# Seven half products for two pairs of column tiles in batch 2's first product and for a second pair of row tiles in batch 0's second product, with w_out's scaling split over two engines

## The chip, the cores and the metric

The kernel runs on one core of a Trainium2 chip. The core has a matrix engine (TensorE, PE in the profile, with its weight loads as PEld), a vector engine (VectorE, DVE), a scalar engine (ScalarE, ACT), GpSimd (POOL) and an engine that mostly issues transfers (SyncE, SP). Each engine works through its own instructions in the order in which they were issued to it, and waits on semaphores for the others. PE writes to PSUM, DVE and ACT read it. The metric is the device time of one execution in microseconds, lower is better; a version counts as faster or slower when it differs by more than 2%.

## What is computed

Four batches of 768 positions, 8 heads of 64: a local attention (16 positions each way, plus 24 block summaries with the maximum of the keys and the mean of the values), and on its output, as 3072 rows of 512, a feed-forward layer with a swish whose slope is given per channel.

```
k_sum = k.reshape(B, H, nb, block, D).max(axis=3)
v_sum = v.reshape(B, H, nb, block, D).mean(axis=3)
scores_l = where(|i - j| < 16, scale * q @ k.T, -1e9)
scores_s = scale * q @ k_sum.T + log(block)
a = softmax(concat(scores_l, scores_s))
x = (a @ concat(v, v_sum)) as rows of 512        # 4 x 768 rows
h = x @ w_in                                     # 512 -> 2048: the first product
g = h * sigmoid(beta * h)
out = g @ w_out                                  # 2048 -> 512: the second product
```

## The kernel before

The kernel takes the batches one after the other. For a batch b it forms the attention (scores, exp on ACT, a mask on DVE, the product with the values, a division on DVE), turns the result into `xT` (512 channels as 4 groups of 128 rows by 768 positions), makes the first product into `h_sb` (16 column tiles of 128 by 768) with the swish on ACT, and then the second product, whose rows go out in tiles of 128. Everything is bf16 with sums in f32. `w_out_sb` is scaled once by 1/beta (`scale_w_out`, 16 pieces of 128x512), since ACT's Silu is given beta*h.

A full column tile of the first product is 8 matmuls of 384 positions (4 channel groups by 2 halves of the positions). `h_some` (operation `c` of the list LAST: tile, PSUM place, first and last channel group) issues them, and `cs` its Silu. A pair of column tiles can instead be made by seven half products in place of eight (`P`), each of two matmuls: sums of quarters of `xT` (`xs`, `x_sums`) and of quarters of `w_in_sb` (`ws`, `w_in_sums`, which also overwrites one quarter) take the place of the operands, and DVE puts the products together in PSUM (`p1`, `u2`, `u3`, `c22`, `c21`, `c12`). The dictionary SEVEN says for which pairs of which batch this is done. Before, these are the pairs 3 and 5 (column tiles 6, 7, 10 and 11) in batch 3 alone.

A row tile of the second product is either 16 matmuls of 512 columns (`o_atom`, four at a time, for batch 0's row tiles 0, 3, 4 and 1), or a pair of row tiles t and t+3 is made by seven half products of 8 matmuls of 256 columns (`half_products`, `product`, `gather`; batch 0's pair t=2, and all three pairs of the other batches). For these, `w_sums` forms sums of `w_out_sb` once, and `h_sums` (`hs`) sums of `h_sb` for each batch; DVE, ACT and POOL put the results together.

The order of the work is written out by hand. `main` is a list of steps of PE work: 8 pairs of column tiles of batch 0's first half (`h_two`), 16 tiles of its second half (`h_half`), the steps of its second product, and then for each later batch 16 steps of the first product (`h_step`, each a sixteenth of the list LAST) and 21 of the second. Everything else stands in the table AT, which gives each piece a place between the steps: loads (`kl`, `ql`, `vl`), DMA transposes on SP's queue (`kd`, `qd`), key windows and key maxima (`win`, `kx`, `ks`), scores (`sc`), masks (`mk`), the products with the values (`av`) and the transposes into `xT` on ACT's queue (`xd`). ENG says which engine makes a copy (d DVE, a ACT, p POOL). So the table fixes the order on each engine; how long a piece waits, it does not say.

PSUM has eight banks: `one` (two single ones), `big[1]` and `big[2]` (two banks each), and a pair that is `big[0]` in the first product and two single accumulators in the second.

## Time and profile before

| | us |
|---|---|
| median of 3 runs (207.07 to 209.65) | 207.76 |
| the profiled execution's own time | 207.91 |
| its span in the trace | 206.2 |
| PE busy | 198.1 |
| DVE busy | 139.0 |
| ACT busy | 126.8 |
| POOL busy | 79.4 |

The profile is of one execution. Its page gives the busy time of each engine, the span in 40 slices, the DMA queues, the chain of work that ended last, and the costliest groups of instructions; behind it stands the trace, which answers for stretches of time, tiles and engines. In the chain a row is the start, the time and the line; in a timeline, the start, the busy time, the engine, the operation with its operands and their count, and in brackets the idle time before it and what ended that.

### The profile page before, as it was taken

What the parts mean: (1) busy time and instruction counts of PE and PEld (TensorE: products, weight loads), DVE (VectorE), ACT (ScalarE), POOL (GpSimd) and SP (SyncE); (2) the same over time, 40 slices, a digit from 0 to 9 for tenths busy, and PEclk for the clock granted to TensorE, in tenths of its full rate; (3) what the DMA queues carried; (4) which work ended last, traced back from release to release, by engine and by line L of the source; (5) the groups of instructions that cost most, each with busy time, mean ns of one, the idle gap of its engine ahead of it and who ended that gap; (6) DMA issues with size and microseconds to landing.
All of it is one profiled execution on the core that took longest, in us unless ns stands there. A gap on an engine that the chain in (4) does not pass through costs nothing.

```text
span 206.2 us, 5853 instructions
## 1 busy us (share of the span) xinstructions
PE 198.1 (96%) x2420; PEld 139.5 (68%) x2424; DVE 139.0 (67%) x327; ACT 126.8 (61%) x197; POOL 79.4 (38%) x112
## 2 busy tenths in 40 slices
PE   7799999999999999999999999999999999999993
PEld 2577766665555775666887866657888866568882
DVE  4567555799979950779799522589789475797132
ACT  2279686588787116767986139668895457792210
POOL 7976992402970049600093379601201100000011
PEclk9999999999999999999999999999999999999999
DMA  6999999999996849999799999999524620000222
GB/s 115 186 172 196 207 206 203 206 193 156 141 180 78 205 98 157 147 137 150 127 185 116 181 153 195 155 156 167 116 105 110 151 103 0 0 3 0 102 101 105
DMA packets 86794, 28.17 MB, mean 137 GB/s; under 512 B 75232, under 2 KB 83824, under 8 KB 86768
## 3 DMA queue, kind: packets, MB, share of 16 engines
...
## 4 chain that ended last, share of the span: by engine, by line
PE 83%; DMA 7%; DVE 4%; issue 3%; POOL 2%; POOLq 0%
PE big L674 21%; PE one L755 15%; PE acc L755 10%; PE one L706 7%; PE one L674 5%; PE big L602 5%; DMA xT<-xn 4%; PE one L608 4%; DMA qrow<-in_q_dram 3%; PE big L462 3%; PE big L647 2%; PE big L415 2%; PE big L534 2%; PE big L608 2%; PE big L449 1%
## 5 line engine op out<-in xcount | busy, mean ns | idle before, releaser
L674 PEld LDWEIGHTS <-w_in_sb 128*128 128x128 bf16 x352 | 34.4, 98 | 22.9 <-issue 0.5
L674 PE MATMUL big<-xT,w_in_sb 128*128 128x384 bf16 x280 | 47.5, 326 | 0.3 <-DMA xT<-xn 0.3
L664 ACT ACTIVATE h_sb<-big,beta_sb 128x768 bf16<-128x768 f32 x39 | 34.6, 901 | 20.2 <-PE big L674 18.7
L736 POOL TENSOR_TENSOR o_sb<-p,u 128x256 f32<-128x256 f32 x10 | 7.3, 725 | 79.8 <-DVE u L736 59.9
L755 PEld LDWEIGHTS <-h_sb 128*128 128x128 bf16 x320 | 30.6, 98 | 4.5 <-issue 0.2
L755 PE MATMUL one<-w_out_sb,h_sb 128*128 128x256 bf16 x240 | 30.2, 273 | 0.2 <-ACT o_sb L393 0.2
L470 ACT ACTIVATE e<-big,bias 128x768 bf16<-128x768 f32 x32 | 27.3, 900 | 4.1 <-PE big L462 2.2
L755 PEld LDWEIGHTS <-s_sb 128*128 128x128 bf16 x240 | 23.2, 98 | 2.8
L736 DVE TENSOR_TENSOR u<-one,p 128x256 f32<-128x256 f32 x20 | 8.4, 422 | 18.1 <-PE one L755 18.0
L399 POOL COPY kw<-km 128x288 bf16<-128x288 bf16 x12 | 7.1, 596 | 34.2 <-DVE km L386 23.0
L253 POOL DMA_DIRECT2D ve<-in_v_dram x15 | 17.1, 1172 | 4.3 <-PE one L929 3.2
L706 PE MATMUL one<-w_out_sb,h_sb 128*128 128x512 bf16 x61 | 14.5, 380 | 0.4 <-issue 0.3
L474 DVE TENSOR_TENSOR e<-e,mask 128x768 bf16<-128x768 bf16 x24 | 12.9, 563 | 1.8 <-ACT e L470 1.6
L674 PE MATMUL one<-xT,w_in_sb 128*128 128x384 bf16 x72 | 14.0, 326 | 0.0
L393 ACT COPY o_sb<-one 128x256 f32<-128x256 f32 (+1 forms) x14 | 6.0, 432 | 12.6 <-PE one L755 7.8
L736 DVE TENSOR_TENSOR s_sb<-h_sb 128x768 bf16<-128x768 bf16 (+2 forms) x15 | 7.6, 508 | 9.2 <-ACT h_sb L682 7.1
L592 POOL DMA_DIRECT2D qn<-in_q_dram x16 | 13.4, 872 | 0.0
L592 POOL DMA_DIRECT2D kn<-in_k_dram x16 | 13.3, 856 | 0.0
L561 DVE TENSOR_TENSOR xn<-big,r 128x768 bf16<-128x768 f32 x12 | 11.5, 958 | 0.4
L386 DVE TENSOR_REDUCE km<-kT 128x24 bf16<-128x768 bf16 x12 | 11.2, 945 | 0.7 <-ACT kT L393 0.6
L602 PE MATMUL big<-xT,w_in_sb 128*128 128x384 bf16 x64 | 11.4, 326 | 0.0
L755 PE MATMUL acc<-t_sb,h_sb 128*128 128x256 bf16 x80 | 10.9, 273 | 0.0
...
## 6 DMA issues: line engine op xcount, KB each, us to landing
...
ve<-in_v_dram POOLq DMA_DIRECT2D x14, 208.0 KB, 12.7
...
```

The lines of the kernel that those rows point to most:

```text
L253: nc.gpsimd.dma_start(out=ve[:, g, 0:n, 0:D], in_=bass.AP(src.tensor, src.offset - W * D, [[D, P], [P * D, n], [1, D]]))
L470: nc.scalar.activation(out=e[:], in_=s[:, :, 0:HS], func=ACTF.Exp, bias=bias[:, 0:1], scale=scale)
L474: eng_of(ENG[f"mk{b}"][2 * g + u]).tensor_mul(out=e.rearrange("p h (m q) -> p h m q", q=QT), in0=e.rearrange("p h (m q) -> p h m q", q=QT) ...
L561: nc.vector.tensor_mul(out=x[:, 3 * us[0]:3 * us[0] + 3 * n].rearrange("p (k j) h d -> p k (j h) d", k=n), in0=tv[:, :, :, 0:D], in1=r[:, ...
L592: nc.gpsimd.dma_start(out=t[:, :, h], in_=pair(k if nm == "k" else q, b, g)[h].rearrange("(j p) d -> p j d", p=P))
L602: nc.tensor.matmul(t[:, 0:HS], w_in_sb[:, ki, i * P:(i + 1) * P], xT[:, ki, 0:HS], start=(ki == 0), stop=(ki == k1 - 1))
L608: nc.tensor.matmul(t[:, 0:HS], w_in_sb[:, ki, i * P:(i + 1) * P], xT[:, ki, lo:lo + HS], start=(ki == 0), stop=(ki == k1 - 1))
L664: nc.scalar.activation(out=h_sb[:, i, :].rearrange("p (k m) -> p k m", k=2), in_=t[:, :, 0:HS], func=ACTF.Silu, scale=beta_sb[:, i:i + 1])
L674: nc.tensor.matmul(o, w_in_sb[:, ki, i * P:(i + 1) * P], x, start=(ki == 0), stop=(ki == k1 - 1))
L706: nc.tensor.matmul(t[:, 0:hi - lo], h_sb[:, n, ms * P:(ms + 1) * P], w_out_sb[:, n, lo:hi], start=(n == 0), stop=(n == k2 - 1))
L736: eng.tensor_tensor(out=o, in0=a, in1=b, op=op)
L755: nc.tensor.matmul(SLOTS[n], a[:, j, t * P:(t + 1) * P], b[:, j], start=(j == 0 and n not in (2, 3, 7)), stop=(j == J2 - 1), skip_group_ch ...
```

## The change

Three things change, and with them most numbers of AT.

Batch 2's first product gets the pairs 3 and 5 by seven half products, as batch 3 has them. `w_in_sums`, which ran at the start of batch 3, moves into batch 1's list, behind column tile 12. LAST[2] is a new list, which also holds DVE's and POOL's work on the keys of batch 3 (`kw`, `kx`, `ks`, that stood in AT). The third sum of `h_sums` for batch 2 moves into its second product (`hz2`).

In batch 0's second product the row tiles 1 and 4 are no longer made by `o_atom`, but as a second pair (t=1) by seven half products. `h_sums` for batch 0 covers 256 columns in place of 128 and stands in eight pieces. Its result `s_sb` and OPERANDS are made at the start, since it is needed before the head's tiles are given back.

Of the 16 scalings of `w_out_sb`, 7 go to POOL. Some copies of batch 0 and 1 change their engine: one group of key windows, one `xT` copy and one query copy from DVE to ACT, two copies of key maxima from POOL to DVE.

```diff
-    'scale': [8.3, 16.158, 16.833, 21.634],
+    'scale': [14.35, 8.574, 20.331, 22.721],
...
-    'exp1': [23.6],
+    'exp1': [27.302],
...
-    'ks2': [57.494, 58.64, 61.796, 70.807],
+    'ks2': [62.273, 71.221, 58.389, 61.875],
...
-    'kw1': 'dddd', 'qt1': 'ddaa', 'x0': 'dd', 'ks1': 'pppp', 'scale': 'd' * 16, 'oc': 'aaaa',
+    'kw1': 'ddad', 'qt1': 'adaa', 'x0': 'ad', 'ks1': 'pddp', 'scale': 'dppdppdpddpddpdd', 'oc': 'aaaa', 'vm1':
...
     2: [
-        ('c', 0, 2, 0, 2), ('c', 2, 1, 0, 2), ('c', 3, 3, 0, 2), ('c', 1, 0, 0, 2), ('c', 0, 2, 2, 3),
...
+        ('c', 1, 2, 0, 2), ('c', 3, 1, 0, 1), ('xs', 3), ('c', 3, 1, 1, 2), ('c', 8, 3, 0, 2), ('c', 8, 3, 2,
+        3), ('c', 3, 1, 2, 3), ('c', 1, 2, 2, 3), ('xs', 0), ('c', 5, 0, 0, 1), ('c', 5, 0, 1, 2), ('c', 1, 2,
...
-SEVEN = {1: {}, 2: {}, 3: {3: (2, 1), 5: (0, 1)}}
+SEVEN = {1: {}, 2: {3: (2, 1), 5: (0, 1)}, 3: {3: (2, 1), 5: (0, 1)}}
...
+        elif name == "kw":
+            windows_nat(cp_of(ENG[f"win{b + 1}"][args[0]]), args[0])
+        elif name == "kx":
+            key_max_nat(args[0])
+        elif name == "ks":
+            key_sums(cp_of(ENG[f"ks{b + 1}"][args[0]]), args[0])
...
-    main.extend([lambda ms=ms, a=a: o_atom(0, ms, a) for ms in (0, 3, 4, 1) for a in range(4)])
-    products(0, (2,))
+    main.extend([lambda ms=ms, a=a: o_atom(0, ms, a) for ms in (0, 3) for a in range(4)])
+    products(0, (1, 2))
...
-    at("hs0", [lambda i=i: h_sums(0, J2, 2 * P, (i,)) for i in range(4)])
+    at("hs0", [lambda i=i, h=h: h_sums(4 * h, 4 * h + 4, P, (i,)) for h in range(2) for i in range(4)])
+    at("hz2", [lambda h=h: h_sums(4 * h, 4 * h + 4, 0, (2,)) for h in range(2)])
```

Batch 0's second product has eight steps of `main` with atoms fewer and seven with half products more, so batch 1 begins at step 46 in place of 47; most places of batches 2 and 3 move by one with it. One number of `ks2` changes what is computed: head pair 1's key maxima of batch 2 are copied into `kw` at 71.221, behind the scores that read them (66.132 and 66.349), so these scores use the 24 maxima that batch 1 left there.

Four places show how rows move on the engines. The first is ACT at the end of batch 0's first product: `qn` are batch 1's queries, `o_sb` a finished row tile, `e` the exponentials of the scores, and the table load with the dummy is the change to the exponential's table. Before:

```order
L826 ACT_TABLE_LOAD
L826 ACTIVATE dummy<-bias 128x1
L393 COPY qn_162<-big_82 128x768
L393 COPY qn_163<-big_82 128x768
L393 COPY o_sb<-one_75 128x512
L470 ACTIVATE e<-big_78,bias 128x768
L470 ACTIVATE e<-big_77,bias 128x768
```

On the same engine at the same place, after:

```order
L395 COPY qn_160<-big_77 128x768
L395 COPY qn_162<-big_82 128x768
L395 COPY qn_163<-big_82 128x768
L395 COPY o_sb<-one_75 128x512
L835 ACT_TABLE_LOAD
L835 ACTIVATE dummy<-bias 128x1
L472 ACTIVATE e<-big_78,bias 128x768
```

The table load moved behind the query copies and the first finished row tile, directly ahead of the first exponential.

The second place is DVE in the second half of batch 0's first product (`km` are key maxima, `t_sb` the sums of `w_out_sb`). Before:

```order
L382 TENSOR_REDUCE km_121<-kw_110 128x24
L362 TENSOR_SCALAR w_out_sb<-w_out_sb,inv_beta 128x512 x4
L382 TENSOR_REDUCE km_122<-kw_111 128x24
L362 TENSOR_SCALAR w_out_sb<-w_out_sb,inv_beta 128x512 x8
L382 TENSOR_REDUCE km_123<-kw_112 128x24
L382 TENSOR_REDUCE km_124<-kw_113 128x24
L736 TENSOR_TENSOR t_sb<-w_out_sb 128x2048
```

After:

```order
L384 TENSOR_REDUCE km_122<-kw_111 128x24
L398 COPY kw_111<-km_122 128x12x24
L364 TENSOR_SCALAR w_out_sb<-w_out_sb,inv_beta 128x512 x2
L384 TENSOR_REDUCE km_124<-kw_113 128x24
L364 TENSOR_SCALAR w_out_sb<-w_out_sb,inv_beta 128x512 x3
L745 TENSOR_TENSOR s_sb<-h_sb 128x4x256
L364 TENSOR_SCALAR w_out_sb<-w_out_sb,inv_beta 128x512 x3
L384 TENSOR_REDUCE km_123<-kw_112 128x24
L398 COPY kw_112<-km_123 128x12x24
L745 TENSOR_TENSOR t_sb<-w_out_sb 128x2048
```

Seven scalings are gone from it, two copies of key maxima and the first sum of `h_sb` stand between the others.

The third place is POOL in the same stretch; `ve` are batch 1's values, `kn` batch 2's keys. Before:

```order
L253 DMA ve<-in_v_dram 128x13x64 x4
L327 AFFINE_SELECT mask<-mask 128x64
L329 MEMSET mask 24x768
L399 COPY kw_110<-km_121 128x12x24
L399 COPY kw_111<-km_122 128x12x24
L399 COPY kw_112<-km_123 128x12x24
L399 COPY kw_113<-km_124 128x12x24
L592 DMA kn<-in_k_dram 128x6x64 x8
```

After:

```order
L255 DMA ve<-in_v_dram 128x13x64 x2
L364 TENSOR_SCALAR w_out_sb<-w_out_sb,inv_beta 128x512 x3
L255 DMA ve<-in_v_dram 128x13x64
L401 COPY kw_110<-km_121 128x12x24
L364 TENSOR_SCALAR w_out_sb<-w_out_sb,inv_beta 128x512 x2
L401 COPY kw_113<-km_124 128x12x24
L364 TENSOR_SCALAR w_out_sb<-w_out_sb,inv_beta 128x512 x2
L594 DMA kn<-in_k_dram 128x6x64 x8
```

The seven scalings stand between the loads and the copies, three of them ahead of the last load of values.

The fourth place is POOL in batch 1's second product; `kn` and `qn` are batch 3's keys and queries, the sums into `o_sb` belong to the row tile pairs t=0, 1 and 2. Before:

```order
L736 TENSOR_TENSOR o_sb<-p_1884,u_1936 128x256
L399 COPY kw_113<-km_124 128x12x24
L592 DMA kn<-in_k_dram 128x6x64 x6
L736 TENSOR_TENSOR o_sb<-p_2077,u_2177 128x256
L592 DMA kn<-in_k_dram 128x6x64 x2
L736 TENSOR_TENSOR o_sb<-p_2282,u_2311 128x256
L592 DMA qn<-in_q_dram 128x6x64 x8
```

After:

```order
L745 TENSOR_TENSOR o_sb<-p_1926,u_1978 128x256
L401 COPY kw_111<-km_122 128x12x24
L594 DMA kn<-in_k_dram 128x6x64 x4
L745 TENSOR_TENSOR o_sb<-p_2118,u_2216 128x256
L594 DMA kn<-in_k_dram 128x6x64 x4
L745 TENSOR_TENSOR o_sb<-p_2324,u_2353 128x256
L594 DMA qn<-in_q_dram 128x6x64 x8
```

Two of the loads of keys moved behind the sum of the pair t=1.

111 lines of the change are left out of this document (54 added, 57 removed), and 73 rows, old and new, of tables (ENG, LAST).

## The prediction

> **What bounds the kernel now.** I read the page first, then each stage by windows, the chain of waits, and the timelines of single engines at the places that the change touches.
>
> ```profile
> span 206.2 us, 5853 instructions
> PE 198.1 (96%) x2420; PEld 139.5 (68%) x2424; DVE 139.0 (67%) x327; ACT 126.8 (61%) x197; POOL 79.4 (38%) x112
> PE 83%; DMA 7%; DVE 4%; issue 3%; POOL 2%; POOLq 0%
> ```
>
> PE is busy for 96% of the span and carries 83% of the chain: time goes where PE loses or saves it. Two windows, batch 0's second product and batch 1's first, tell how much room the others have.
>
> ```profile
> 48.00:75.00 27.00, 26.61 (x406) 16.56 (x408) 24.19 (x46) 16.39 (x26) 9.95 (x12) 1.00 1.20 145
> 75.00:100.00 25.00, 25.00 (x188) 16.11 (x186) 14.87 (x31) 17.02 (x22) 11.78 (x14) 1.00 1.74 148
> ```
>
> The columns are the length, then PE, PEld, DVE, ACT and POOL busy, the granted clock (1.00) and DMA. From 48 to 75 us DVE works 24.19 of 27: it is almost as full as PE. From 75 to 100 it has 10 us free.
>
> **The work that PE is spared.** Rows of the chain of waits (start, time, line):
>
> ```profile
> 52.30 1.83 PE one L706 x8
> 54.13 0.46 PE big L462 x24
> ...
> 58.71 0.51 PE big L509 x28
> ...
> 72.71 1.75 PE one L755 x16
> ...
> 75.33 1.30 PE big L674 x8
> ...
> 114.85 7.99 DMA xT<-xn
> ...
> 125.64 15.60 PE big L674 x96
> ...
> 164.31 0.65 PE one L674 x4
> ...
> 184.48 0.77 PE acc L755 x7
> ```
>
> A matmul of 512 columns (L706) takes 1.83/8 = 0.229 us, one of 256 (L755) 1.75/16 = 0.109, one of the first product (L674) 15.60/96 = 0.1625. Row tiles 1 and 4 of batch 0 cost 32 x 0.229 = 7.32 us; as seven half products they cost 56 x 0.109 = 6.12. That spares 1.20. Two pairs of column tiles are 32 matmuls; by seven half products 28, which spares 4 x 0.1625 = 0.65. That such pairs can run without holes is seen in batch 3: from 164.31 to 184.48 are 20.17 us, and 124 x 0.1625 = 20.15. So the most that these edits can spare PE is 1.85 us.
>
> **Batch 2's start: the 0.65 is waited away.** The timeline of PE there:
>
> ```profile
> 119.82 1.46 PE L674 MATMUL big<-xT,w_in_sb 128*128 128x384 bf16 x8
> 121.12 0.81 PE L674 MATMUL one<-xT,w_in_sb 128*128 128x384 bf16 x4
> 121.77 0.81 PE L674 MATMUL big<-xT,w_in_sb 128*128 128x384 bf16 x4
> 122.88 2.11 PE L674 MATMUL big<-xT,w_in_sb 128*128 128x384 bf16 x12 [0.29 <-DMA xT<-xn]
> ```
>
> PE does 16 matmuls that need channel groups 0 and 1 alone, 2.60 us, and then waits 0.29 for the third group's transpose, the one of 7.99 us in the chain. The new list has 12 such matmuls (tiles 1, 3 and 8) ahead of the first that needs group 2: 12 x 0.1625 = 1.95. The transpose comes out of batch 1's second product, whose steps keep their places to one another, so it lands as long after that product's start as before, and the wait becomes 0.29 + 0.65 = 0.94. Behind the landing both lists have the same PE work, 128 - 16 = 124 - 12 = 112 matmuls. So this edit counts -0.65 and +0.65.
>
> What it adds on DVE is covered, by these groups (DVE's additions in PSUM, and one of the four `w_in_sums` in the timeline):
>
> ```profile
> L736 DVE TENSOR_TENSOR big<-big,o_sb 128x384 f32<-128x384 f32 x6 | 3.4, 565 | 0.6 <-PE big L647 0.5
> ```
>
> ```profile
> 164.78 0.42 DVE L736 TENSOR_TENSOR wsum<-w_in_sb 128x512 bf16<-128x512 bf16 x1
> ```
>
> The sums of `xT` (`xs`) need all four groups and hold DVE's queue until these have landed; behind them stand the sums of the first pair, whose products come later still, and the Silu of tiles 1, 3, 8 and 5 are on ACT, so nobody waits for the held queue. Two pairs need ten additions of 0.57 in PSUM, and with batch 3's keys and the sums of `h_sb` DVE is full for nearly the whole stage. Batch 3 has a like list without a hole: I take 0, between 0 and the 1.1 of two additions by which it may come late. The moved `w_in_sums`, 4 x 0.42, fall into the 10 us that DVE has free from 75 to 100: 0, and at most their 1.7.
>
> **Batch 0's second product: the 1.20 is partly given back.** ACT around its table load:
>
> ```profile
> 49.55 1.28 ACT L826 ACT_TABLE_LOAD   x1
> 50.84 0.20 ACT L826 ACTIVATE dummy<-bias 128x1 f32<-128x1 f32 x1
> ...
> 54.16 0.58 ACT L393 COPY o_sb<-one 128x512 f32<-128x512 f32 x1 [0.33 <-PE one L706]
> 54.65 1.70 ACT L470 ACTIVATE e<-big,bias 128x768 bf16<-128x768 f32 x2
> ```
>
> The load of 1.28 us stood in time in which ACT waited for PE anyway. Now it stands behind the copy of the first row tile: 54.16 + 0.58 + 1.28 + 0.20 = 56.2, and the first exponential ends at 57.1 (0.85 each). PE comes to the third scores, which need its PSUM, at 54.13 + 0.46 + 8 x 0.229 + 0.51 = 56.9. It waits about 0.3. Bounds: 0, and 1.28 for the whole load; the small end is nearer, since both times are summed from rows.
>
> DVE in the same stage, and the two rows of POOL that stood beside it:
>
> ```profile
> 40.21 1.13 DVE L362 TENSOR_SCALAR w_out_sb<-w_out_sb,inv_beta 128x512 bf16<-128x512 bf16 x4
> 41.26 2.68 DVE L396 COPY kw<-big 128x960 bf16<-128x960 bf16 x4
> ...
> 44.71 1.31 DVE L362 TENSOR_SCALAR w_out_sb<-w_out_sb,inv_beta 128x512 bf16<-128x512 bf16 x4
> ...
> 50.79 1.21 DVE L736 TENSOR_TENSOR t_sb<-w_out_sb 128x2048 bf16<-128x2048 bf16 x1
> 51.92 1.80 DVE L396 COPY qn<-big 128x768 bf16<-128x768 bf16 x2
> ...
> 72.20 0.68 DVE L736 TENSOR_TENSOR h_sb<-h_sb 128x1024 bf16<-128x1024 bf16 x1
> 72.80 0.42 DVE L736 TENSOR_TENSOR u<-one,p 128x256 f32<-128x256 f32 x1
> ...
> 74.95 0.84 DVE L736 TENSOR_TENSOR o_sb<-acc,u 128x256 f32<-128x256 f32 x2
> ```
>
> ```profile
> 44.93 0.42 POOL L399 COPY kw<-km 128x288 bf16<-128x288 bf16 x1 [6.48 <-DVE km L382]
> ...
> 50.93 1.36 POOL L399 COPY kw<-km 128x288 bf16<-128x288 bf16 x1 [0.43 <-DVE km L382]
> ```
>
> Ahead of the first `t_sb`, DVE loses seven scalings of 0.28 (2.0) and one of two groups of key windows (1.3), and gains a sum of `h_sb` (0.6) and two copies of key maxima (POOL's 0.42 each at most; 0.3 by my estimate). So it starts about 2.1 us earlier. From there to `u` of the pair t=2 it gains four sums (2.4, at 0.60 from start to start) and the gathering of t=1 (0.42 + 0.42 + 0.84), and loses a query copy (0.9): about 3 more. So `u` ends near 73.2 - 2.1 + 3 = 74.1, or up to 2 us earlier if DVE no longer waits for anybody in this stretch: 72.1 to 74.1, by the middle 73.1. PE needs it for the last but one product of t=2, two products (1.75 us) ahead of batch 1, at 75.33 - 1.20 + 0.3 - 1.75 = 72.7. That is a wait of 0.4 (0 to 1.4). [...] Of POOL's seven scalings three stand beside DVE's copies out of PSUM, two beside its reductions, two beside scalings. I add 0.18 for each of the last two, but half of that, since some of DVE's lost time comes out of waits: 0.2, and 0.6 for DVE in all.
>
> POOL's scalings are also ahead of the last load of values and of batch 2's keys in POOL's queue. Those loads land late anyway; the last one of values, issued at 36.2:
>
> ```profile
> ve<-in_v_dram POOLq DMA_DIRECT2D x1, 208.0 KB, 16.5
> ```
>
> With 16.5 us it waited in the queue behind weights and queries, so some us of later issue leave its landing where it was: 0.
>
> **The sum.** 207.91 - 1.20 - 0.65 + 0.65 + 0.3 + 0.6 = 207.6 for an execution such as the profiled one, which lies 0.15 above the median of the runs: 207.4.
>
> **The rivals.**
>
> *All of it comes.* The transposes into `xT` around 155 to 161 us, with no loads of keys beside them, landed so:
>
> ```profile
> DMA to landing us min/median/max: 2.7/2.8/3.5
> ```
>
> And those of batch 1's second product so:
>
> ```profile
> DMA to landing us min/median/max: 3.1/5.5/8.0
> ```
>
> If the third one lands 1 us earlier, the 0.65 and the 0.29 come back: 206.4; with DVE and ACT on time too, 205.6. Against it: nothing beside the transposes gets lighter.
>
> *The transposes land later: slower.* POOL's rows there:
>
> ```profile
> 113.02 0.72 POOL L736 TENSOR_TENSOR o_sb<-p,u 128x256 f32<-128x256 f32 x1 [3.46 <-issue]
> 113.70 1.69 POOL L592 DMA_DIRECT2D kn<-in_k_dram  x2
> ```
>
> Two loads of keys (1.69 us of issuing) ran beside the third transpose, issued at 114.85; now four do. If the two more hold it up by their own length, batch 2 starts 1.7 later: 207.4 + 1.7 = 209.1. It decides from 0.4 us on, where the 207.8 of before is passed. For it: the transposes are slow only where these loads are.
>
> *POOL's scalings block DVE whole: slower.* A scaling on POOL lasts about 0.75 us by its copy (0.42/288 x 512). If the four beside DVE's reductions and scalings each hold DVE for that long, 3.0 us in place of 0.2, DVE is the bound there: 207.4 + 2.8 = 210.2. It decides from 0.15 us each on. [...]
>
> *It does nothing in sum:* ACT and DVE give back the whole 1.20: 207.8, inside the forecast's own range.
>
> **How the numbers follow.** The forecast, with its own range of 206.5 to 208.4 (both waits 0; DVE's at 1.4), gets 0.5; all of it comes 0.2; late transposes 0.15; blocked DVE 0.1; 0.05 for what I don't see, such as keys or queries of batch 2 that land late in their new order. The time is that of the likeliest, 207.4. To hold it 8 times in 10 the range takes in most of the first rival and the late transposes: 205.8 to 209.3. A measurement of this kernel can tell about 2% (4.2 us) from no change. Faster by that is 203.6, below all that PE is spared: 0.02. Slower by that is 211.9, both slower rivals at once: 0.03. Within: 0.95.
>
> **What would show it.** In the changed kernel's profile: 32 matmuls fewer in the atoms' group and a batch 0 that ends 0.3 to 0.9 earlier; batch 2's first product with a wait of about 0.9 for `xT` after 12 matmuls and no hole behind it; holes of some tenths on PE between 56 and 73 us that end with ACT's `e` and DVE's `u`. The forecast is wrong if the third transpose lands within 6 us of its issue or takes over 9, if PE's busy time falls by less than 1.5 us, or if DVE's scalings and sums between 43 and 50 us grow by more than 1 us in all.

## The result and the profile after

The changed kernel takes 217.91 us in the median of 4 runs (215.39 to 218.97), the kernel before 208.0 beside it: 1.0427 times as long, with a 95% interval of 1.0302 to 1.0551. It is slower, and lies outside the range of the prediction (205.8 to 209.3). Ratios, here and in the table below, leave out the executions that are over 1.5% above the fastest of their kernel, such as the 218.97 here, while medians are of all. The profiled execution took 217.34 us. The page of the changed kernel:

```profile
span 215.6 us, 5914 instructions
PE 200.8 (93%) x2440; PEld 142.7 (66%) x2444; DVE 147.9 (69%) x332; ACT 128.9 (60%) x204; POOL 89.4 (41%) x118
...
PE 49%; DVE 22%; DMA 18%; issue 4%; POOL 3%; ACT 1%; SPq 0%; ACTq 0%; POOLq 0%; DVEq 0%
```

PE was busy for 96% of the span and is now busy for 93%; of the chain of waits it carried 83% and now carries 49%. So PE waits, and DVE and transfers have come into the chain. Where, the windows tell, cut at the first matmul of each stage. For before (length, then PE, PEld, DVE, ACT and POOL busy, clock, DMA):

```profile
48.93:75.17 26.24, 25.87 (x402) 16.28 (x405) 23.43 (x42) 15.58 (x24) 10.06 (x13) 1.00 1.15 144
...
95.97:119.82 23.85, 23.31 (x389) 19.82 (x388) 18.38 (x42) 15.61 (x27) 9.29 (x13) 1.00 1.18 155
119.82:141.08 21.26, 20.97 (x131) 12.51 (x128) 10.88 (x21) 14.52 (x18) 12.71 (x16) 1.00 1.80 162
141.08:164.15 23.07, 23.07 (x390) 19.65 (x388) 17.82 (x43) 16.69 (x27) 3.04 (x6) 1.00 0.68 132
```

And the same four stages after (batch 0's second product, batch 1's second, batch 2's first and second):

```profile
48.67:78.11 29.44, 27.13 (x425) 19.18 (x428) 26.65 (x52) 15.94 (x24) 9.36 (x12) 0.94 0.98 121
...
98.91:126.42 27.51, 24.97 (x390) 20.56 (x388) 21.76 (x50) 15.90 (x27) 8.80 (x12) 0.94 0.81 130
126.42:149.97 23.55, 20.79 (x126) 12.11 (x124) 15.12 (x27) 14.63 (x22) 14.77 (x18) 1.00 1.85 161
149.97:173.56 23.59, 23.48 (x390) 19.75 (x388) 20.44 (x42) 15.49 (x27) 1.49 (x3) 1.00 0.64 117
```

They are longer by 3.20, 3.66, 2.29 and 0.52, together 9.7. The first of them began 0.26 earlier, and the span grew by 9.4. Two of the four also have a granted clock of 0.94. The other stages are as long as before. PE's waits of over 1 us in them, from the timeline of PE (in brackets the wait and what ended it):

```profile
56.02 0.48 PE L464 MATMUL big<-qn,kw 64*128 64x64 bf16 x12 [1.87 <-DVE qn L398]
...
103.36 0.53 PE L464 MATMUL big<-qn,kw 64*128 64x64 bf16 x24 [2.54 <-DVE kw L398]
...
129.96 0.48 PE L676 MATMUL one<-xT,w_in_sb 128*128 128x384 bf16 x2 [1.42 <-DMA xT<-xn]
...
141.01 0.49 PE L649 MATMUL big<-e,w_in_sb 128*128 128x384 bf16 x2 [1.15 <-ACT h_sb L666]
```

The waits in batch 0 and 1 cost more than their length. Windows of 2 us (the same columns) show the clock at half for some 4 us behind each:

```profile
56.00:58.00 2.00, 1.65 (x15) 0.76 (x15) 2.00 (x4) 1.58 (x3) 1.14 (x2) 0.52 1.57 224
58.00:60.00 2.00, 2.00 (x33) 1.00 (x32) 1.01 (x4) 0.00 (x0) 0.00 (x0) 0.63 1.78 200
...
104.00:106.00 2.00, 2.00 (x11) 1.40 (x10) 1.93 (x6) 1.44 (x2) 0.00 (x0) 0.50 0.59 135
106.00:108.00 2.00, 2.00 (x14) 1.53 (x13) 1.57 (x4) 0.37 (x1) 0.00 (x0) 0.68 0.45 106
```

**What is late in batch 0.** Rows of DVE's timeline after, up to the query copy:

```profile
39.95 0.71 DVE L364 TENSOR_SCALAR w_out_sb<-w_out_sb,inv_beta 128x512 bf16<-128x512 bf16 x1
...
44.33 1.70 DVE L364 TENSOR_SCALAR w_out_sb<-w_out_sb,inv_beta 128x512 bf16<-128x512 bf16 x2
...
46.81 1.46 DVE L364 TENSOR_SCALAR w_out_sb<-w_out_sb,inv_beta 128x512 bf16<-128x512 bf16 x3
...
48.80 1.31 DVE L364 TENSOR_SCALAR w_out_sb<-w_out_sb,inv_beta 128x512 bf16<-128x512 bf16 x3
...
51.35 1.16 DVE L745 TENSOR_TENSOR t_sb<-w_out_sb 128x2048 bf16<-128x2048 bf16 x1
52.61 2.48 DVE L745 TENSOR_TENSOR t_sb<-w_out_sb,t_sb 128x2048 bf16<-128x2048 bf16 x2
55.02 0.95 DVE L398 COPY qn<-big 128x768 bf16<-128x768 bf16 x1
```

Nine scalings took 5.18 us where 9 x 0.28 = 2.5 was DVE's price before, and two sums of 1.24 stand ahead of the copy that PE waits for: the second scores go to the PSUM bank in which the transposed queries still lie. POOL's row beside them gives 1.56 us for one scaling:

```profile
37.40 4.68 POOL L364 TENSOR_SCALAR w_out_sb<-w_out_sb,inv_beta 128x512 bf16<-128x512 bf16 x3 [0.56 <-DMA w_out_sb<-in_moe_w_out_dram]
```

**What is late in batch 1.** The chain of waits (start, time, line) and, below, SP's own queue in the timelines, before and after:

```profile
91.29 0.86 DVE km L388
...
92.18 5.86 DMA kT<-kn
...
98.07 0.46 DVE kw L398
...
103.36 0.53 PE big L464 x24
```

```profile
77.35 4.69 SPq L596 DMA_TRANSPOSE kT<-kn  x3
```

```profile
80.56 12.84 SPq L598 DMA_TRANSPOSE kT<-kn  x3
93.56 3.75 SPq L598 DMA_TRANSPOSE qn<-qn  x2
97.36 1.28 SPq L598 DMA_TRANSPOSE kT<-kn  x1
```

```profile
SPq L598 <- DVE s_sb L745: 9.5, 1, 9.5
```

Three transposes of keys take 4.69 us on SP before and 12.84 after. In the table of waits one of them waits 9.5 us for DVE. The cause stands in the change's numbers: pair 1's maxima (`kx2`, 51.576) come ahead of its transpose (`kd2`, 52.012). So the reduction at 91.29 reads the old keys, the transpose may overwrite them only afterwards, and everything behind it on SP is late.

The order also changes more of what is computed than the one number of `ks2` named above. Pair 1's maxima are taken from the keys that `kT` still holds, and the copies of pairs 2 and 3 (`ks2` 58.389 and 61.875) stand ahead of their reductions (`kx2` 58.488 and 61.978), so they take the maxima that batch 1 left. POOL makes three of the four copies in one go, where DVE's reductions of these two pairs follow only at 101.24 and 104.99:

```profile
91.06 1.25 POOL L401 COPY kw<-km 128x288 bf16<-128x288 bf16 x3
```

### The profile page after: what moved, and what is told of

Read it like the earlier page. It is cut to its first block, busy times and chain, and to the rows that moved or that the text cites. A ratio compares the mean times of both kernels' runs of the same rounds, so it can differ in the third digit from the quotient of the medians.

```text
span 215.6 us, 5914 instructions
## 1 busy us (share of the span) xinstructions
PE 200.8 (93%) x2440; PEld 142.7 (66%) x2444; DVE 147.9 (69%) x332; ACT 128.9 (60%) x204; POOL 89.4 (41%) x118
## 4 chain that ended last, share of the span: by engine, by line
PE 49%; DVE 22%; DMA 18%; issue 4%; POOL 3%; ACT 1%; SPq 0%; ACTq 0%; POOLq 0%; DVEq 0%
PE one L764 13%; DMA kT<-kn 10%; PE acc L764 9%; PE big L604 5%; DVE s_sb L745 5%; PE one L676 4%; DMA qrow<-in_q_dram 3%; PE big L676 3%; DVE kw L398 3%; DMA qn<-in_q_dram 2%; DVE w_out_sb L364 2%; DMA xT<-xn 2%; PE big L649 2%; PE one L714 2%; DVE km L388 2%
## 5 line engine op out<-in xcount | busy, mean ns | idle before, releaser
L676 PEld LDWEIGHTS <-w_in_sb 128*128 128x128 bf16 x320 | 31.3, 98 | 22.3 <-issue 2.0
L666 ACT ACTIVATE h_sb<-big,beta_sb 128x768 bf16<-128x768 f32 x35 | 30.8, 901 | 19.9 <-PE big L676 15.3
L676 PE MATMUL big<-xT,w_in_sb 128*128 128x384 bf16 x216 | 37.5, 326 | 0.1
L764 PEld LDWEIGHTS <-h_sb 128*128 128x128 bf16 x352 | 33.6, 98 | 4.9
L764 PE MATMUL one<-w_out_sb,h_sb 128*128 128x256 bf16 x264 | 33.4, 273 | 0.0
L676 PE MATMUL one<-xT,w_in_sb 128*128 128x384 bf16 x104 | 20.3, 326 | 1.4 <-DMA xT<-xn 1.4
L388 DVE TENSOR_REDUCE km<-kT 128x24 bf16<-128x768 bf16 x12 | 11.2, 946 | 10.2 <-DMA kT<-kn 9.2
L684 ACT ACTIVATE h_sb<-one,beta_sb 128x384 bf16<-128x384 f32 x26 | 14.0, 582 | 1.7 <-PE one L676 1.5
L764 PE MATMUL one<-t_sb,s_sb 128*128 128x256 bf16 x88 | 12.3, 286 | 0.0
L764 PE MATMUL acc<-t_sb,s_sb 128*128 128x256 bf16 x88 | 12.3, 286 | 0.0
L764 PE MATMUL acc<-w_out_sb,s_sb 128*128 128x256 bf16 x88 | 11.4, 273 | 0.0
## 6 DMA issues: line engine op xcount, KB each, us to landing
ve<-in_v_dram POOLq DMA_DIRECT2D x14, 208.0 KB, 8.6
```

The lines of the kernel that those rows point to most:

```text
L388: nc.vector.tensor_reduce(out=km[g][:, NK:NK + nb], in_=kT[g][:, W:W + S].rearrange("p (n f) -> p n f", f=block), op=ALU.max, axis=AX.X)
L666: nc.scalar.activation(out=h_sb[:, i, :].rearrange("p (k m) -> p k m", k=2), in_=t[:, :, 0:HS], func=ACTF.Silu, scale=beta_sb[:, i:i + 1])
L676: nc.tensor.matmul(o, w_in_sb[:, ki, i * P:(i + 1) * P], x, start=(ki == 0), stop=(ki == k1 - 1))
L684: nc.scalar.activation(out=h_sb[:, i, kk * HS:(kk + 1) * HS], in_=one[kk][:, 0, 0:HS], func=ACTF.Silu, scale=beta_sb[:, i:i + 1])
L764: nc.tensor.matmul(SLOTS[n], a[:, j, t * P:(t + 1) * P], b[:, j], start=(j == 0 and n not in (2, 3, 7)), stop=(j == J2 - 1), skip_group_ch ...
```

## The experiments

The stages as in the windows above, and the medians (before as measured beside each, 207.9 to 208.2):

| kernel | batch 0, 2nd | batch 1, 2nd | batch 2, 1st | batch 2, 2nd | median | ratio, 95% |
|---|---|---|---|---|---|---|
| before | 26.24 | 23.85 | 21.26 | 23.07 | 208.0 | |
| after | 29.44 | 27.51 | 23.55 | 23.59 | 217.9 | 1.030 to 1.055 |
| kd_first | 30.75 | 23.49 | 22.45 | 23.59 | 215.0 | 1.022 to 1.037 |
| ws_behind_q | 28.29 | 25.45 | 23.21 | 23.59 | 215.9 | 1.024 to 1.040 |
| scale_dve | 28.00 | 24.80 | 22.37 | 23.59 | 213.5 | 1.018 to 1.031 |
| undo_seven2 | 27.98 | 27.15 | 21.56 | 23.35 | 214.4 | 1.022 to 1.038 |
| only_batch0 | 28.09 | 23.26 | 22.21 | 23.07 | 212.9 | 1.011 to 1.026 |
| mend_batch0 | 26.70 | 23.25 | 22.66 | 23.07 | 209.8 | 1.003 to 1.011 |
| nomask_batch0 | 26.23 | 23.24 | 21.77 | 23.07 | 208.7 | 0.998 to 1.006 |
| pairs_batch0 | 26.70 | 23.25 | 23.05 | 24.05 | 210.2 | 1.004 to 1.016 |
| only_keys2 | 26.24 | 24.98 | 22.66 | 23.07 | 211.0 | 1.009 to 1.021 |
| only_seven2 | 26.24 | 23.26 | 23.60 | 23.55 | 211.7 | 1.010 to 1.022 |
| seven2_keys_out | 26.24 | 23.26 | 25.94 | 24.42 | 212.3 | 1.015 to 1.027 |
| seven2_nokeys | 26.23 | 23.26 | 21.57 | 23.40 | 208.5 | 0.999 to 1.004 |
| seven2_keys_last | 26.24 | 23.25 | 22.02 | 30.05 | 216.0 | 1.031 to 1.041 |
| seven2_mended | 26.24 | 24.63 | 20.19 | 29.97 | 214.2 | 1.022 to 1.030 |
| seven2_fit | 26.24 | 23.83 | 20.69 | 24.41 | 209.1 | 1.003 to 1.008 |
| kl3_alone | 26.24 | 23.76 | 21.63 | 23.06 | 209.3 | 1.001 to 1.006 |
| mend_all | 26.69 | 30.05 | 25.49 | 24.42 | 218.7 | 1.037 to 1.049 |

The stages are of one profiled execution each.

### First, one thing at a time undone in the changed kernel

**kd_first.** The key transpose ahead of the maxima that read it:

```diff
-    'kd2': [46.896, 52.012, 49.287, 53.919],
+    'kd2': [46.896, 51.5, 49.287, 53.919],
```

> The changed kernel with one number moved: head pair 1's key transpose for batch 2 (kd2) at 51.5 instead of 52.012, so that it is issued ahead of the key maxima of the same pair (51.576). The order on every engine stays the same; what changes is who waits: before this edit the transpose on SP's queue waits for DVE's read of the old keys, and the maxima of that pair are those of batch 0's keys. Theory C (this wait holds SP's queue for 9.5 us and makes batch 1's second product late): the third key transpose is issued near 83 us instead of 93, DVE's wait of 2.54 for the key windows and PE's 2.54 for the scores at 103.4 vanish, with the half clock behind it; the kernel takes 217.9 - 2.5 to 3.7 = 214.2 to 215.4. Rival (DVE has too much in batch 1's first product: w_in's sums and the sums of h_sb crowd out the windows): DVE's queue stays as late, PE still waits over 1.5 us, and the time stays above 216.5.

215.02 us (213.54 to 215.83). SP's queue and PE at the place, from its timelines:

```profile
82.59 4.52 SPq L598 DMA_TRANSPOSE kT<-kn  x3
```

```profile
58.49 0.50 PE L464 MATMUL big<-qn,kw 64*128 64x64 bf16 x12 [3.26 <-DVE qn L398]
...
103.39 0.53 PE L464 MATMUL big<-qn,kw 64*128 64x64 bf16 x24 [0.18 <-DMA qn<-qn]
```

The three transposes are out by 87.1, and PE's 2.54 became 0.18. Batch 1's second product takes 23.49, less than before the change, and the time is in theory C's range. So one number, and the wait that it made on SP, is the whole loss of this stage: theory C holds. The other row tells that batch 0's wait differs from run to run with the same instructions: 1.87, here 3.26.

**ws_behind_q.** Two sums of `w_out_sb` behind the query copy:

```diff
-    'ws': [23.767, 23.768, 24.034, 31.733],
+    'ws': [23.767, 25.6, 26.6, 31.733],
```

> The changed kernel with the second and third sum of w_out (ws) at 25.6 and 26.6 instead of 23.768 and 24.034, as before: the second copy of batch 1's queries stands behind one of these sums on DVE instead of three. Theory B (the order on DVE: two sums of 1.24 us ahead of the copy that frees the bank for the second scores): PE's wait of 1.87 at 56 us falls under 0.4, the clock stays at 1.00 from 56 to 60 us, and the kernel takes 217.9 - 1.9 to 3.6 = 214.3 to 216.0. Theory A (POOL's scalings are what makes DVE late): the wait moves to what stands behind, and the time falls by less than 1: over 216.9.

215.89 us (214.06 to 218.4), at the upper end of theory B's range. The wait for the query copy is gone, but two new ones have come at 66 us, and batch 0's stage is still 28.29 us:

```profile
66.40 0.22 PE L536 MATMUL big<-ve,e 128*64 128x65 bf16 x1 [0.70 <-DVE e L476]
68.08 0.22 PE L536 MATMUL big<-ve,e 128*64 128x65 bf16 x1 [1.30 <-DVE e L476]
```

These are the masks, DVE's next work, which now has the two sums ahead of it. So the wait for the copy was made by the order, but two waits of together 2.00 took its place. That the time lies in theory B's range is in part luck: the profiled execution gains 1.15 us in batch 0 and 2.06 in batch 1's second product, which the edit doesn't touch. There PE waits 2.15 for the same copy of key windows, and its clock stays at 1.00 behind it.

**scale_dve.** No scaling on POOL:

```diff
-    'scale': 'dppdppdpddpddpdd'
+    'scale': 'dddddddddddddddd'
```

> The changed kernel with all 16 scalings of w_out on DVE. DVE gets seven scalings of 0.28 (2.0 us) back and loses what POOL's cost it: its own nine scalings took 5.2 us instead of 2.5. Theory A (POOL's scalings make DVE late): t_sb starts 1 us earlier or more, the wait at 56 us falls by as much, and the time falls by 1 to 3 us: 214.9 to 216.9. Theory B (the order on DVE makes it late): t_sb starts within 1 us of 51.35, PE still waits 1.0 to 2.7 us, and the time stays within 1 us: 216.9 to 218.9.

213.54 us (213.11 to 214.7), faster than either theory said. The first sum of `w_out_sb` starts at 51.98, 2.2 us behind the stage's start (after: 2.7, before: 1.9), and PE still waits:

```profile
56.58 0.35 PE L489 MATMUL big<-qn,kw 64*128 64x64 bf16 x12 [1.33 <-DVE qn L423]
```

By t_sb and the wait theory B is right, by the time neither. Its 16 scalings take DVE 5.19 us, as long as the nine beside POOL's (5.18): what POOL took off it, POOL cost it again. Much of the rest is the clock, which stays at 1.00 in all four stages of the profiled execution. Batch 0's second product is 1.44 us shorter, batch 2's first 1.18, and batch 1's second 2.71, where PE's wait for the key windows is 1.49 in place of 2.54 and no half clock follows:

```profile
101.96 0.53 PE L489 MATMUL big<-qn,kw 64*128 64x64 bf16 x24 [1.49 <-DVE kw L423]
```

The transpose on SP is held there too (three take 11.93 us), so this part of the gain is no sign for either theory.

**undo_seven2.** Batch 2's first product as before:

```diff
-SEVEN = {1: {}, 2: {3: (2, 1), 5: (0, 1)}, 3: {3: (2, 1), 5: (0, 1)}}
+SEVEN = {1: {}, 2: {}, 3: {3: (2, 1), 5: (0, 1)}}
...
-    'win3': [],
+    'win3': [90.341, 92.68, 90.196, 99.991],
```

> The changed kernel with batch 2's first product made as before (no half products, the old list, batch 3's keys at their old places, w_in's sums back in batch 3), everything else as changed. Theory D (the new list costs 2.8 us from batch 2's start to its end, where it was to cost nothing): 217.9 - 2 to 3.5 = 214.4 to 215.9, with no wait on PE from 131 to 150 us and one of about 0.3 to 0.8 for xT. Rival (what is lost there is handed down from batch 1, whose transposes come late): the time stays above 217.

214.44 us (213.95 to 216.15), in theory D's range. In the profiled execution batch 2's two products are 1.99 and 0.24 shorter than after the change, and PE waits 0.44 for `xT`; another 1.46 is gained in batch 0, which the edit doesn't touch. So the third part costs by itself, at its own place, about 2.2 us.

### Then, one part alone on the kernel before

In these kernels (and in mend_batch0, nomask_batch0, pairs_batch0, seven2_keys_out, seven2_nokeys and seven2_keys_last) batch 3's four key loads stand one step later against the steps of batch 1, as in the change; kl3_alone, below, prices that. The diffs show the main lines of each edit only.

**only_batch0** (second pair, its places and engines), **only_keys2** (the numbers of batch 2's keys, queries and values) and **only_seven2** (batch 2's first product):

```diff
-    main.extend([lambda ms=ms, a=a: o_atom(0, ms, a) for ms in (0, 3, 4, 1) for a in range(4)])
-    products(0, (2,))
+    main.extend([lambda ms=ms, a=a: o_atom(0, ms, a) for ms in (0, 3) for a in range(4)])
+    products(0, (1, 2))
```

```diff
-    'kd2': [47.896, 48.564, 50.287, 53.981],
-    'kx2': [50.116, 57.618, 60.611, 66.447],
+    'kd2': [47.896, 53.012, 50.287, 54.919],
+    'kx2': [49.237, 52.576, 59.488, 62.978],
```

```diff
-SEVEN = {1: {}, 2: {}, 3: {3: (2, 1), 5: (0, 1)}}
+SEVEN = {1: {}, 2: {3: (2, 1), 5: (0, 1)}, 3: {3: (2, 1), 5: (0, 1)}}
```

> The kernel before with the first part of the change alone: batch 0's second pair with its places, engines and the split scaling; the keys of batch 2 at the places of before and batch 2's first product as before. If batch 0's second product is what it was in the changed kernel (28.0 to 30.8 us from its first matmul to batch 1's, where 26.24 stood before) and the rest is as before, the time is 208.0 + 1.8 to 4.5 = 209.8 to 212.5. If the loss there comes from what else was changed, it is under 209.

> The kernel before with the second part alone: the numbers of batch 2's keys, queries and values (ql2, vl2, kd2, win2, kx2, ks2, qd2, vo2, exp2) as in the changed kernel; batch 0 and batch 2's first product as before. As in the changed kernel the key maxima of pair 1 are taken ahead of its transpose (from batch 0's keys), those of pairs 2 and 3 are copied ahead of their reduction, and pair 1's copy comes behind its scores. Theory C (the transpose on SP waits for that read and holds SP's queue): SP's third key transpose stands 6 to 10 us behind the second, DVE waits 1.5 us or more for the key windows behind it, batch 1's second product takes 24.8 to 27.5 us (before 23.85), and the kernel 208.2 + 1.0 to 3.7 = 209.2 to 211.9. Rival (it takes w_in's sums on DVE in batch 1 as well): 207.9 to 208.9.

> The kernel before with the third part alone: batch 2's first product with two pairs of column tiles by seven half products, its new list with batch 3's keys in it, w_in's sums moved into batch 1's list. My prediction counted this at nothing. In the three runs above where it stood, batch 2's first product took 22.4 to 23.2 us (before 21.26) and its second 23.59 (before 23.07). Theory D (the list itself costs it): 208.0 + 1.1 to 2.5 = 209.1 to 210.5, with a wait of 0.9 to 1.5 for the third group of xT. If it is only hurt by what batch 1 hands down late: 207.7 to 208.6.

212.89 (+4.7), 210.96 (+3.1) and 211.66 us (+3.4) against before beside them. Each part alone takes longer than before: the three intervals lie above 1, though none wholly above 2%. The first and the third are over the range that was given, the second is inside theory C's. The three sum to 11.2; since all hold the later key loads (0.7, below), twice 0.7 goes off: 9.8, where the whole change costs 9.9. So no loss is seen that only the parts together make, as far as medians of four runs tell. In only_keys2 SP's three transposes take 11.61 us, in only_seven2 PE waits thus:

```profile
134.43 0.48 PE L673 MATMUL big<-e,w_in_sb 128*128 128x384 bf16 x2 [1.60 <-ACT h_sb L690]
```

DVE's rows ahead of it tell why: a window copy waits 1.96 us for its key transpose, and the two sums in PSUM that ACT needs stand behind it.

```profile
131.54 0.57 DVE L422 COPY kw<-kT 128x1152 bf16<-128x1152 bf16 x1 [1.96 <-DMA kT<-kn]
132.03 0.93 DVE L412 TENSOR_REDUCE km<-kT 128x24 bf16<-128x768 bf16 x1
132.89 1.01 DVE L769 TENSOR_TENSOR big<-big,o_sb 128x384 f32<-128x384 f32 x2
```

The profiled run of only_batch0 was its fastest (209.97; the others 212.8 to 213.0), so its stages show only some 2 us of the loss.

### Batch 0: order, volume, or PE itself

**mend_batch0**, on only_batch0:

```diff
-    'ws': [23.767, 23.768, 24.034, 31.733],
+    'ws': [23.767, 25.6, 26.6, 31.733],
...
-    'exp1': [27.302],
+    'exp1': [23.8],
...
-    'qt1': 'adaa',
+    'qt1': 'aaaa',
...
-    'scale': 'dppdppdpddpddpdd',
+    'scale': 'dddddddddddddddd',
...
-    'vm1': 'dddd',
+    'vm1': 'dada',
```

> The run above with DVE relieved: all scalings on DVE again (no POOL scalings beside it), the second and third sum of w_out behind the query transposes, all four query copies and half of the copies of the means on ACT, and the exponential's table loaded ahead of the query copies. Theory V (DVE's volume bounds batch 0's second product: it was busy 26.2 of 28.0 us): about 1.5 us of DVE work leave, the stage takes 26.2 to 27.0 us, and the kernel 208.0 to 208.8. Theory B (only the order of the query copy made the loss): the stage takes about 25.3, PE's work alone, and the kernel 207.1.

**nomask_batch0**, on that:

```diff
-        at("mk" + n, [lambda g=g, u=u, b=b: mask_e(b, g, u) for g in range(G) for u in range(2)])
+        if b > 1:
+            at("mk" + n, [lambda g=g, u=u, b=b: mask_e(b, g, u) for g in range(G) for u in range(2)])
```

> The run above without the eight multiplications of batch 1's exponentials with the mask (left out: batch 1's local window is not cut to 16 positions on each side). DVE is spared 8 x 0.5 = 4 us between 55 and 73 us. Theory V: batch 0's second product loses its last waits and takes 25.0 to 25.6 us, so the kernel is 0.6 to 1.8 faster than the run above and 0.5 to 1.2 faster than before. Rival (what is left of the loss is PE's own, from changing more often between scores, products and values): the stage stays within 0.4 us of the run above.

The stage takes 26.70 us in mend_batch0, in theory V's range; the kernel, 209.8, is over it, and in its trace PE also loses 0.9 in batch 1's first product, where it waits for `xT`. nomask_batch0 leaves out the masks of batch 1's local attention, so it computes something else. There the stage takes 26.23, where V said 25.0 to 25.6 and the rival no change of more than 0.4: 0.47 shorter, nearly as the rival has it. Its window shows that nobody but PE is left:

```profile
51.25:77.48 26.23, 25.94 (x428) 18.60 (x428) 21.00 (x40) 16.34 (x27) 7.28 (x10) 1.00 0.95 126
```

PE works 25.94 of 26.23 us, and DVE has 5 us free. So of the spared 1.20 no more than 0.3 is there for anybody to give back. Where the rest went, the starts of the rows tell. Before, and then in nomask_batch0:

```profile
56.81 1.90 PE L706 MATMUL one<-w_out_sb,h_sb 128*128 128x512 bf16 x8
58.64 0.58 PE L509 MATMUL big<-ve,A_avg 128*32 128x128 bf16 x28
```

```profile
56.84 1.04 PE L736 MATMUL one<-w_out_sb,h_sb 128*128 128x512 bf16 x4
57.81 0.58 PE L533 MATMUL big<-ve,A_avg 128*32 128x128 bf16 x28
```

Eight matmuls of an atom in a row take 1.83 us from start to start, but four take 0.97 and not 0.92. A half product takes 0.88 when another one follows and 0.97 when scores or values follow. The 24 matmuls of a pair of scores take 0.46 in one go, and 2 x 0.28 when other work stands between the halves. So in these rows each change from one kind of work to another costs PE 0.05 to 0.1 us. In sum, the 32 matmuls of the atoms take 7.53 (32 x 0.229 = 7.32), the 14 half products 12.57 (14 x 0.875 = 12.25), and everything else 6.13 with the wait of 0.29 (before 5.6, where two records of atoms are missing from the trace). That is 0.2, 0.3 and 0.2 more than priced. Both rows of the prediction were short of what lies between groups.

**pairs_batch0**, mend_batch0 with the scores two by two as before:

```diff
-    'sc1': [27.303, 27.729, 29.212, 31.973, 31.223, 30.064, 34.796, 34.969],
+    'sc1': [27.05, 27.06, 29.05, 29.06, 31.06, 31.07, 34.05, 34.06],
```

> The relieved run of batch 0's second pair (209.8) with batch 1's scores two at a time, at the places of before, instead of one by one. In the run without masks, where PE waited for nothing but 0.29, the stage still took 26.23 us where 25.0 was expected: summed from its rows, the atoms took 0.2 more than 32 x 0.229, the scores, values and transposes 0.3 more than before, the half products 0.3 more than 14 x 0.875. Theory S (each change of PE from one kind of work to another costs 0.05 to 0.09 us, and the pair with its scattered scores makes some ten more of them): with the scores in pairs the stage takes 26.0 to 26.5 in place of 26.70. Theory V (DVE's volume): it stays at 26.6 to 27.2 with DVE's or ACT's waits in it. By both, the time stays within 0.7 of 209.8 less the other waits: 208.6 to 209.9.

The stage again takes 26.70, with a wait of 0.44 for ACT and 0.28 for DVE in it, as theory V said. Theory S is not borne out by the stage's time, but it is by PE's rows: without the waits the stage is 25.98, in mend_batch0 26.13 (waits 0.29 and 0.28). The two groups fewer spare 0.15, and ACT's wait grows by as much. The time, 210.19 (208.93 to 211.76), is over its range.

### Batch 2: order or volume on DVE

**seven2_keys_out**: only_seven2 with batch 3's keys out of the list and at the places of before.

```diff
-    'win3': [],
+    'win3': [91.341, 93.68, 91.196, 100.991],
...
-        ('u2', 3), ('c', 9, 3, 0, 4), ('u3', 3), ('c', 0, 0, 0, 2), ('c', 0, 0, 2, 4), ('c22', 3), ('kw', 0),
+        ('u2', 3), ('c', 9, 3, 0, 4), ('u3', 3), ('c', 0, 0, 0, 2), ('c', 0, 0, 2, 4), ('c22', 3),
```

> The run with the third part alone, with batch 3's key windows, maxima and copies taken out of batch 2's list and back at the places of before. In that run PE waited 1.60 us at 134.4 for a Silu on ACT that waited for a sum on DVE, behind a copy of key windows that waited for their transpose. Theory D1 (the place of the keys in the list makes this wait): the wait falls under 0.4, batch 2's first product takes 22.0 us or less in place of 23.6, and the kernel 211.7 - 1.2 to 2.2 = 209.5 to 210.5. Theory D2 (DVE has too much there, wherever the keys stand): the wait moves to another sum or into batch 2's second product, and the time stays within 0.8: over 210.9.

212.32 us (211.51 to 213.96): the wait moved, as D2 said. Now three window copies stand ahead of the second pair's sums and wait 1.87 and 0.58 us for their transposes, and PE waits longer:

```profile
138.26 0.48 PE L673 MATMUL big<-e,w_in_sb 128*128 128x384 bf16 x2 [2.29 <-DVE o_sb L769]
```

**seven2_nokeys** (`kw`, `kx` and `ks` out of LAST[2] and nowhere else) and **seven2_keys_last** (all twelve behind the last sum):

```diff
-        2, 3), ('c12', 5), ('c', 15, 1, 3, 4), ('c', 14, 3, 0, 2), ('cs', 13), ('hs', 0, 5, 0), ('sx', 5),
+        2, 3), ('c12', 5), ('kw', 0), ('kx', 0), ('ks', 0), ('kw', 2), ('kx', 2), ('ks', 2), ('kw', 1), ('kx', 1),
+        ('ks', 1), ('kw', 3), ('kx', 3), ('ks', 3), ('c', 15, 1, 3, 4), ('c', 14, 3, 0, 2), ('cs', 13),
```

> The run with the third part alone (211.7; batch 2's first product 23.6 us with waits of 0.75 and 0.48 for xT and 1.60 behind DVE), with batch 3's key windows, key maxima and their copies left out: batch 3's scores read batch 2's windows, so its output is another. Theory D1 (a key copy that waits for its transpose holds the sums behind it on DVE): the wait of 1.60 vanishes, the first product takes 21.4 to 22.2, and the kernel 209.4 to 210.4. Theory D2 (the ten additions and w_in's and xT's sums themselves are too much for DVE there): a wait behind DVE of 0.8 us or more stays, and the time is over 210.8.

> The same run with the keys computed, but all of them behind the last sum of the two pairs in batch 2's list, so that no copy that waits for a transpose stands ahead of a sum in PSUM. Theory D1: no wait behind DVE in the first product from its third us to its 18th, 21.4 to 22.2 us for it; the sums of h_sb come later by 4 x (0.46 + 0.95) = 5.6 us of DVE work, so its second product may take 23.5 to 24.5; the kernel 209.6 to 211.4. Theory D2: over 211.4, with waits of more than 0.8 us behind the sums of the pairs.

Without keys 208.52 us (207.89 to 211.25), as fast as before: the ten additions, and the sums of `xT` and `w_in_sb`, cost nothing by themselves, and the time is even under D1's range. But this run also takes 5.6 us of work off DVE, so alone it doesn't tell order from volume. With the keys last, 215.97 us (214.23 to 216.82): no wait for DVE in the first product, but 7.0 us more in the second, where PE waits for the sums of `h_sb` that now come 5.6 us later, and its granted clock falls to half (0.50 in the three windows from 148 to 154 us):

```profile
147.91 1.25 PE L790 MATMUL one<-t_sb,s_sb 128*128 128x256 bf16 x5 [2.92 <-DVE s_sb L771]
```

So the order decides where PE waits, and the volume leaves little choice of it.

**kl3_alone**, the kernel before with later key loads:

```diff
-    'kl3': [75.5, 74.5, 72.5, 73.5],
+    'kl3': [76.5, 75.5, 73.5, 74.5],
```

> The kernel before with batch 3's four key loads one step later, as they stand in the changed kernel and in all runs with a part of it; nothing else is moved, and it alone differs on POOL: two loads behind the second gathering instead of ahead of it. My rival in the prediction (four loads beside the third transpose into xT instead of two let it land later): it lands 7.5 to 9 us after its issue, batch 2's first product waits 0.9 to 1.6 instead of 0.29, batch 1's second product takes 23.3 instead of 23.85, and the kernel 0.0 to 0.8 more than before. If the loads don't matter: the wait stays under 0.5 and the time within 0.3.

209.25 us (208.1 to 211.6), 1.0035 times before (1.0010 to 1.0061): 0.7 us (0.2 to 1.3). The wait for `xT` is 0.60 in place of 0.29:

```profile
123.02 2.17 PE L697 MATMUL big<-xT,w_in_sb 128*128 128x384 bf16 x12 [0.60 <-DMA xT<-xn]
```

**seven2_mended**: seven2_keys_last with the key loads of before and tile 5's first four matmuls in front; **seven2_fit**: the same with the keys spread over DVE's holes.

```diff
-        ('c', 8, 3, 0, 2), ('c', 8, 3, 2, 3),
+        ('c', 8, 3, 0, 2), ('c', 5, 0, 0, 2), ('c', 8, 3, 2, 3),
...
-        ('xs', 0), ('c', 5, 0, 0, 1), ('c', 5, 0, 1, 2),
+        ('xs', 0),
```

```diff
...
+        ('c12', 3), ('kw', 0), ('kx', 0), ('ks', 0),
...
+        ('u3', 5), ('kw', 2), ('kx', 2), ('ks', 2),
...
+        ('c22', 5), ('kw', 1), ('kx', 1), ('ks', 1),
...
+        ('hs', 2, 8, 3), ('kw', 3), ('kx', 3), ('ks', 3),
```

> The third part with three remedies: the keys behind the sums of the pairs, batch 3's key loads at their step of before, and tile 5's four matmuls of the first two channel groups ahead of the first matmul that needs the third (16 instead of 12 stand there, as before). If these are all its losses: the wait for xT under 0.5, the first product 20.6 to 21.2 (before 21.26), the second 23.1 to 24.2, and the kernel from 0.6 less than before to 0.9 more. If DVE's added work must be paid somewhere: more than 1.2 above before.

> The mended third part with batch 3's keys spread over DVE's holes in batch 2's first product: pair 0's window copy and maxima behind the last sum of the first pair of column tiles (hole of 1.66 us), pair 2's behind the first two sums of the second (0.97), pair 1's ahead of its last (1.76), pair 3's behind the sums of h_sb; each takes 0.45 + 0.95 = 1.4 us. Theory order (a place exists where the keys neither wait for their transpose ahead of a sum nor push the sums of h_sb back): first product 20.2 to 21.2, second 23.1 to 24.4, the kernel 207.4 to 209.2. Theory volume (DVE cannot take them beside the ten additions): a wait of over 1 us behind DVE comes back in one of the two products, and the kernel takes over 210.

In seven2_mended batch 2's first product takes 20.19 us, which is 124 x 0.1625 = 20.15: the whole of the spared 0.65 and the 0.29 of before are there, and no wait for `xT`. Part of that is luck: batch 1's second product took 24.63 in this execution (PE waits 1.25 for a copy of values), and no transpose into `xT` landed later than 6.2 us after its issue. Its second product pays 6.9 for the late sums: 214.16 us (212.74 to 214.76). In seven2_fit, with the same 16 matmuls in front, PE waits 0.35 for `xT`; the first product takes 20.69 and the second 24.41, and the kernel 209.07 (208.2 to 210.53), in the range of theory order: 0.57 won, 1.34 paid, 0.5% longer than before (1.0025 to 1.0081).

### All together

**mend_all**: pairs_batch0's edits, kd_first's, seven2_keys_out's and tile 5 in front, in the changed kernel, and

```diff
-    'ks2': [62.273, 71.221, 58.389, 61.875],
+    'ks2': [62.273, 62.3, 58.6, 62.0],
```

> All three parts together with what the runs showed mended: the relieved batch 0 with scores in pairs, the key transpose of pair 1 ahead of its maxima and all copies of maxima behind their reductions (so that batch 2's summaries are those of its own keys again), batch 3's keys out of batch 2's list, and tile 5's first four matmuls ahead of the first that needs the third group of xT. If every loss has been found: batch 0's second product 26.3, batch 1's 23.4, batch 2's first 21.0 to 21.6 and second 23.1 to 23.6; against before 0.1 + 0.4 less and 0 to 0.8 more: 207.5 to 209.0. If DVE's added work costs elsewhere: over 209.5.

218.7 us (216.2 to 220.38). A miss, and the new `ks2` made it. Pair 3's copy of maxima stood ahead of pair 0's on POOL in the change already, but took the old maxima and waited for nothing. Now it waits for its own reduction, and that for pair 3's late transpose:

```profile
98.22 0.48 POOL L426 COPY kw<-km 128x288 bf16<-128x288 bf16 x1 [10.14 <-DVE km L413]
```

PE waits for pair 0's copy behind it:

```profile
102.97 0.82 PE L489 MATMUL big<-qn,kw 64*128 64x64 bf16 x24 [5.08 <-POOL kw L426]
```

The trace is of one of the longest executions (219.7), so it shows the kind of this loss, and its size only there. It is the mistake of the change once more, on another queue. The kernel also had the keys as in seven2_keys_out, with a wait of 2.23 us at its place. No version beat the kernel before, and the three parts were not put together once more with this order mended.

## Why the prediction was wrong

The forecast was 207.4, and the kernel took 217.9. The sum counted the work of each engine. What the four stages lost, 9.7 us, are waits that the new order makes, with half clock behind two of them (0.50 to 0.68 in the windows above), and of the time to be spared in batch 0 three quarters were not there.

**"That spares 1.20" (batch 0).** This step failed. Without any wait but 0.29 (nomask_batch0) the stage is as long as before, 26.23 against 26.24. The prices were means over eight or sixteen matmuls in a row. The new order has more and shorter groups, and the changes between them, some 0.7 us by the rows, were in no term. With the masks, waits for ACT and DVE add up to 0.57, and the stage takes 26.70 at best (mend_batch0).

**"So it starts about 2.1 us earlier", "a wait of 0.4" (DVE in batch 0).** The first `t_sb` came 0.6 later, not 2.1 earlier. Two terms were wrong: a scaling on POOL lasts 1.56 us and not the 0.75 that I took from a copy by its size, and POOL's scalings cost DVE 2.6 us over its own nine, not 0.2. No run shows that 0.2, an estimate of mine from 1.31 us for four scalings beside a copy of POOL's in place of 1.13: the nine beside POOL's scalings took 5.18 in place of 2.5. And I looked for the wait at `u` at the stage's end; it came at the query copy, behind two sums whose numbers the change had moved ahead of it (1.87, gone in ws_behind_q).

**"POOL's scalings block DVE whole" (chance 0.1).** Some of it was there in batch 0, priced at 210.2: 16 scalings on DVE alone take it 5.19 us (scale_dve), as long as nine beside POOL's (5.18). But the rows show no hold of a whole scaling of POOL's (1.55 to 1.59): single scalings of DVE's took 0.34 to 1.02 there (the middle one 0.71, before 0.34), and its reductions 0.94, as before. And it is no more than a part of the loss there, since with it gone PE still waits 1.33 for the query copy.

**"It lands as long after that product's start as before, and the wait becomes 0.29 + 0.65 = 0.94."** The wait was 1.42, and the third transpose took 8.2 us, inside the bounds set for it. The 0.65 is waited away as forecast, and 0.57 of it comes back when 16 matmuls stand ahead again (seven2_fit). The rival of the later landing, priced at 1.7, is real but small: 0.7 (kl3_alone).

**"I take 0, between 0 and the 1.1" (DVE in batch 2).** This step failed too. The additions do cost nothing by themselves (seven2_nokeys), as batch 3 suggested. But I counted what DVE had to do and not what stands behind what: a copy of key windows that waits for its transpose stood ahead of sums that PE needs. I named batch 3's keys only as volume. Alone, the third part costs 3.4 us, 0.7 of it by the later key loads.

**The moved `w_in_sums`: "0, and at most their 1.7".** Right: in only_seven2 they stand in batch 1, and its first product stays 20.8 and its second 23.26. **"The small end is nearer" (table load, 0.3).** In ws_behind_q, with the load still behind the row tile, PE waits for no exponential: 0, within the bounds.

**"0.05 for what I don't see, such as keys or queries of batch 2 that land late in their new order".** This step cost most, 3.66 us of batch 1's second product in the profile, and the order would have shown it: I followed what each engine does in a row, but not which row of one engine another's must wait for. A reduction moved ahead of the transpose of its own input turned the wait around (kd_first takes it away, only_keys2 makes it alone).

Two of the three signs that were to show the forecast wrong are there: PE's busy time rose by 2.7 us, since half clock stretches it (eight matmuls of 256 columns, from 103.82 and 105.50 on, took 1.88 and 1.91 us, and 1.05 at a clock of 1.00), and DVE's scalings and sums between 43 and 50 us take some 5.2 us in place of 3.7. Half clock behind a wait was in no term; in the profile of before the clock is 1.00 in these stages, where no wait is longer than 0.30.

What stays open: why batch 0's part alone costs 4.7 us in its median where its profiled (fastest) execution shows some 2. The edits of mend_batch0 take 3.1 of it away, but no trace of a longer execution is at hand, and half clock alone isn't it, since the execution of 212.78 had a mean granted clock of 1.00.
